# Moving a fused kernel's side work to other steps of its groups, and its agents' halves and key loads to other places

## The chip, the cores and the metric

One core of one Trainium2 chip runs the whole program. The metric is device time in microseconds (us) from the first to the last instruction of one execution, with what lies around them; the median of three runs is the figure for a kernel. TensorE is called PE here, VectorE DVE, ScalarE ACT, GpSimd POOL and SyncE, which issues the transfers, SP.

## What is computed

An attention over 49 agents (keys are folded into the agents, queries then read the agents), followed by a two-matrix layer with a leaky rectifier whose slope `alpha` differs by column. Two batches of 12480 tokens with 128 channels; the layer is 2048 wide.

```python
def attn(q, k, v, agents):                   # q, k, v: 2 x 12480 x 128; agents: 2 x 49 x 128
    a2k = softmax(scale * agents @ k.T)      # over all keys
    agent_v = a2k @ v                        # 49 x 128 per batch
    q2a = softmax(scale * q @ agents.T)      # over the 49 agents
    return q2a @ agent_v

def layer(x, w_in, w_out, alpha):            # w_in 128 x 2048, w_out 2048 x 128
    h = x @ w_in
    g = max(h, 0) + alpha * min(h, 0)
    return g @ w_out
```

## The kernel before

**Halves.** Most products run as sums of pairs of reduced-precision numbers: a value is split into a high part (written by ACT) and the rest (written by DVE as a difference). So `qh` and `ql` are a query group's halves, `ah` and `al` the agents', `rh` and `rl` those of the rectified layer input.

**Start (to about 105 us).** Keys of batch 0 come in 25 units `u` of 512 rows. Each unit is transposed on PE (`ktp`), copied by ACT (`kt`), multiplied with the agents (`kl`), and its scores copied out (`s`). Maxima, exponentials and the product with the values (`av`) follow in five spans of units. Between them DVE turns the weights, which arrive as 64-bit numbers, into 32-bit ones (`mag_win`, `wl` and their like). `prep_agents` (line 152) stands at the head of all this: for both batches it transposes the agents (`ag`) and makes `ah` with 8 copies on ACT and `al` with 4 differences and 4 copies on DVE.

**Loop.** Then 52 groups of 480 tokens follow, each in 8 steps (NM = 8); a step `s` handles 256 of the 2048 layer columns. In step `s` PE runs, in this order, `g1(s + 2)` (6 matmuls into `h`, from which ACT makes `rh` and DVE `rl`), then whatever the plan puts into the step, then `g2(s)` (12 matmuls that add `rh` and `rl` into `acc`). At a group's eighth step three more matmuls add the linear part (`zh`, `zl`), ACT copies one half of `acc` to `os` (line 829) and DVE adds the other (line 830). `h` has two buffers: `g1(s + 2)` overwrites what `rl` of step `s` has read, so it cannot start before that `rl` has ended. ACT, DVE, POOL and SP each run their instructions in the order in which the program states them.

**Shared banks.** Two PSUM bank pairs take turns as `acc`: a group uses one, and `pair_tile` (line 82) lends the other, which the group before has just left, to the work between: a query pair's logits (`lg`), its sums over the agents (`qsum`), the key products of batch 1 (`kl`, `av`), and the fold (`t1` to `ts`). Such a matmul must wait until DVE has added up `os` of the group before.

**The plan.** `at(s, f)` puts a function into step `s` after `g1`, `pre(s, f)` ahead of `g1`. Query groups are made in pairs, one for every 16 steps; `q_steps` (line 960) says at which step, counted from the pair's first, each link of the chain runs (transpose, halves, logits, copy, maximum on POOL, `q_sub` on DVE, two exponentials on ACT, the split, the sum, its way through memory as `qx`, the reciprocal). `hold` (line 981) finds two free steps for a use of the shared bank. Batch 1's keys (`kb`, four transfers a unit, three buffers) and values are spread over the first 26 groups, its fold over the groups after them. In `fold_tasks`, `rest` is the linear part: `tt` (16 matmuls), four `tm`, `tz` (16 matmuls) and `ts`, which makes `zh` and `zl`.

Below, "step 0 to 15" of a pair means its place in the 16 steps: a group ends with step 7, the next begins with step 8.

Of the kernel before, what the change touches and what calls it, by code (L numbers as in the profile page):

```python
# [10 lines left out]
F32R = mybir.dt.float32r  # L11
# [20 lines left out]
def kernel(  # L32
# [11 lines left out]
    nc = tc.nc  # L44
# [18 lines left out]
    NM = NF // 2  # L63
# [14 lines left out]
    TILES = ((0, HALF), (HALF, P))  # L78
# [73 lines left out]
    def prep_agents(b):  # L152
        t = ps_l.tile([P, 512], F32, tag="lg", name=f"agt_ps{b}")
        nc.tensor.transpose(t[:, 0:NA], agm[:, b, :], ident[0:NA, 0:NA])
        ag = per_b.tile([P, HALF], F32, tag="ag", name=f"ag{b}")
        nc.vector.tensor_copy(ag[:, 0:NA], t[:, 0:NA])
        nc.vector.tensor_copy(ag[:, NA:HALF], t[:, 0 : HALF - NA])

        ah, al = (
            per_b.tile([P, 2, 2, HALF], F32R, tag=n, name=f"{n}{b}") for n in ("ah", "al")  # L160
        )
        for h, (c0, c1) in enumerate(TILES):
            for r0, r1 in TILES:
                for d in range(2):
                    nc.scalar.copy(out=ah[r0:r1, h, d, :], in_=ag[c0:c1, :])
            for d in range(2):
                nc.vector.tensor_tensor(
                    out=al[c0:c1, h, d, :], in0=ag[c0:c1, :], in1=ah[c0:c1, h, d, :],
                    op=ALU.subtract,
                )  # L170
                r0, r1 = TILES[1 - h]
                nc.vector.tensor_copy(
                    al[r0:r1, h, d, :].bitcast(F32R), al[c0:c1, h, d, :]
                )
        st[b].update(ag=ag, ah=ah, al=al)

    raw = {}

# [681 lines left out]
    with tc.manual_schedule():  # L860
# [9 lines left out]
        for b in range(B):  # L870
# [3 lines left out]
            out=oma, in0=alp, scalar1=-1.0, scalar2=1.0, op0=ALU.mult, op1=ALU.add  # L874
# [7 lines left out]
        def at(s, f, *a):  # L882
            plan.setdefault(s, []).append((f, a))
# [7 lines left out]
        s = 0  # L891
# [17 lines left out]

        q0 = s - (NU - CUTS[-1])  # L910
        loads += [(q0 - 14, q_load, 0), (q0 - 4, q_load, 1)]
        for j, f in zip((-6, -5, -4, -2, -1, 0, 3, 3, 4, 4), q_chain[:10]):
            at(q0 + j, f, 0)
        for n in range(8):
# [42 lines left out]
        for f, i in zip(rest, (0, 0, 1, 1, 2, 3, 4)):  # L957
            at(i, f)

        q_steps = (-21, -20, -19, -15, -14, -14, -12, -11, -11, -9, -7, -6, -4)  # L960
        load = {}

        first = {}
# [1 line left out]
        def pre(s, f, *a):  # L965
            first.setdefault(s, []).append((f, a))
# [13 lines left out]

        def hold(s):

            while s in busy or s + 1 in busy or s % NM in (0, NM - 1):
                s += 1
            busy.update((s, s + 1))
            return s

        for i2 in range(NGT // 2):
            s0 = 2 * NM * i2
            if i2 == 0:  # L990
                at(9, q_sum, 0)
                pre(10, q_spread, 0)
                at(12, q_rec, 0)
                busy.update((0, 1, 2, 3, 4, 9, 10))
                continue
            steps = q_steps
            if i2 == 1:
                steps = (-14, -14, -13, -11, -10, -10, -8, -7, -7, -6, -5, -4, -3)
            else:
                at(max(0, s0 - 30), q_load, i2)  # L1000
            for i in (3, 10):
                busy.update((s0 + steps[i], s0 + steps[i] + 1))
            for f, i in zip(q_chain, steps):
                (pre if f in (q_take, q_spread) else at)(s0 + i, f, i2)
        for g in range(NGT):
            s0 = g * NM
            for i in range(NM):
                use(s0 + i, "dve", 0.57)
            for i in (7, 7, 0, 1):
                use(s0 + i, "act", 0.5)  # L1010
            at((g + 1) * NM + 3, o_take, g)
            at((g + 1) * NM + 6, o_scale, g)
            at((g + 1) * NM + 7, o_store, g)

        for b in range(1, B):
            base = (b - 1) * NG * NM
            parts = [(u, u + 2) for u in range(0, NU - 3, 2)] + [(NU - 3, NU)]
            assert NU % 2
            at(base + 8, k_begin, b, [(0, NU)], parts)
            s = base + 9  # L1020
            done = {}
            for c, (lo, hi) in enumerate([*parts[:-1], (NU - 3, NU - 1), (NU - 1, NU)]):
                us = tuple(range(lo, hi))
                for u in us:
                    s = fit(max(s, done.get(u - 3, 0) + 1), dve=0.57)
                    at(max(base, s - 9), load_kb, b, u)
                    at(s, k_transpose_dve, b, u)
                    s += 1
                t_log = hold(max(s + 1, done.get(lo - 1, 0) + 2))
                done.update((u, t_log) for u in us)  # L1030
                at(t_log, k_logits, b, us)
                pre(t_log + 1, k_take, b, us)
                use(t_log + 1, "dve", 0.4)
                if hi in (NU, *(p[1] for p in parts)):
                    t_max = fit(t_log + 2, dve=0.4)
                    at(t_max, k_max_keys, b, min(c, len(parts) - 1))
            s = t_max + 1
            at(s, k_max, b)
            s += 3
            done = {}  # L1040
            for lo, hi in parts:
                us = list(range(lo, hi))
                t_av = s
                for u in us:
                    s = fit(s, dve=0.3)
                    at(s, k_exp_a, b, u)
                    t_v = fit(max(s, done.get(u - 4, 0) + 1), act=0.5, dve=0.57)
                    at(max(base, t_v - 8), load_v1, b, u)
                    at(t_v, v_split, b, u)
                    t_e = fit(max(s + 1, done.get(u - 4, 0) + 1), act=0.5)  # L1050
                    at(t_e, k_exp_b, b, u)
                    t_c = fit(t_e + 1, dve=0.3)
                    at(t_c, k_exp_c, b, u)
                    t_av = max(t_av, t_c + 2, t_v + 2)
                t_av = hold(t_av)
                at(t_av, k_av2, b, us)
                pre(t_av + 1, k_add, b, us)
                use(t_av + 1, "dve", 0.5)
                for u in us:
                    done[u] = t_av  # L1060
            s = t_av + 2
            at(s, k_sum, b)
            lead, rest = fold_tasks(b)
            s += 2
            for f in lead:
                s = hold(s)
                at(s, f)
                s += 2
            while s % NM != 3 or any(s + i in busy for i in range(5)):
                s += 1  # L1070
            for f, i in zip(rest, (0, 1, 1, 2, 2, 3, 4)):
                at(s + i, f)
            busy.update(range(s, s + 5))
            s += 4
            assert s < base + (NG + 1) * NM - 1, (t_max, t_av, s, base + NG * NM)

        for s in range(NS):
# [41 lines left out]
```

## Time and profile before

| | us |
|---|---|
| median of three runs (lowest, highest) | 1112.08 (1108.16, 1114.1) |
| the profiled execution | 1114.53 |
| its span, first to last instruction | 1112.7 |
| PE busy in the span | 1059.0 |
| DVE busy | 820.3 |
| ACT busy | 634.1 |

PE is busy for 95% of the span, so the time is PE's own work and the places where it stands still. Matmuls overlap: the two row halves of one product run at once, and a step of 18 matmuls in loop takes about 2 us from one `h` to the next. A row that says `[0.39 <-DVE os L830]` means that the engine sat idle 0.39 us before this instruction and that DVE's line 830 ended the wait. The distance from one step's first `h` to the next shows a loss better than the idle time does, because the matmul pipeline has to fill again.

### The profile page before, as it was taken

To read this page: it belongs to the slowest core of one execution; us is meant where nothing else is said; L and a number is where in the kernel's file an instruction comes from. 1 tells how busy PE (TensorE), PEld (TensorE's weight loads), DVE (VectorE), ACT (ScalarE), POOL (GpSimd) and SP (SyncE) were. 2 spreads that over 40 slices of the span, in tenths; PEclk is the share of its full clock that TensorE was granted. 3 is DMA by queue.
4 is the path that set the end of the run, shared out by engine and by line. 5 is a ranking of instruction groups with operands and counts; after the bars stand their busy time and mean duration, and the time that the engine had idled before them with its cause. 6 is when DMAs were issued, how large, how long until landed. Compare 5 with 4: busy or idle time off the path is not lost.

```text
span 1112.7 us, 22465 instructions
## 1 busy us (share of the span) xinstructions
PE 1059.0 (95%) x9328; PEld 939.9 (84%) x9328; DVE 820.3 (74%) x1068; ACT 634.1 (57%) x807; POOL 109.9 (10%) x130
## 2 busy tenths in 40 slices
PE   7998969999999999999999899999999999999997
PEld 7985858877878878888878789899998899899997
DVE  5696557787786799899877577767777777777775
ACT  3354445555555567767656456666566665666653
POOL 1341101101101100110110110011101111011100
PEclk9989989999999999999999999999999999999999
DMA  9881013313323223233211111021211212112011
GB/s 264 221 185 28 1 31 64 57 30 65 57 39 50 47 57 76 60 73 70 37 28 23 24 29 33 15 37 30 35 29 19 37 28 38 21 27 37 10 20 28
DMA packets 305767, 57.25 MB, mean 51 GB/s; under 512 B 265567, under 2 KB 305153, under 8 KB 305665
## 3 DMA queue, kind: packets, MB, share of 16 engines
q1 hardware_dynamic: 304673, 55.69, 25.7%
q8 instruction: 73, 1.20, 0.4%
q14 instruction: 29, 0.24, 0.1%
q10 hardware_dynamic: 992, 0.12, 0.1%
HBM read 42.59 MB, written 12.78 MB: 50 GB/s over the span
## 4 chain that ended last, share of the span: by engine, by line
PE 62%; DVE 21%; ACT 10%; issue 4%; SPq 1%; DMA 1%; DVEq 0%; ACTq 0%; POOL 0%
PE acc L816 31%; PE h L794 16%; DVE rl L801 7%; ACT rh L800 5%; PE kl L372 4%; PE lg L713 3%; DVE qs L731 2%; ACT qmh L735 2%; ACT qs L740 2%; DVE qml L744 2%; PE av L527 2%; DVE ot L840 2%; DVE os L830 1%; PE qsum L755 1%; PE ktp L340 1%
## 5 line engine op out<-in xcount | busy, mean ns | idle before, releaser
L801 DVE SCALAR_TENSOR_TENSOR rl<-h,rh 128x960 fp32r<-128x960 f32 x416 | 476.5, 1150 | 236.4 <-ACT rh L800 235.7
L800 ACT ACTIVATE rh<-h 128x960 fp32r<-128x960 f32 x416 | 402.1, 971 | 322.6 <-PE h L794 314.2
L794 PE MATMUL h<-qmh,sab 64*128 64x480 f32 x1664 | 363.9, 384 | 5.9 <-DVE rl L801 4.9
L816 PE MATMUL acc<-rh,wl 64*128 64x480 f32 x1664 | 361.3, 382 | 1.5 <-DVE zl L663 1.2
L816 PE MATMUL acc<-rh,wh 64*128 64x480 f32 x1664 | 358.8, 378 | 0.0
L816 PE MATMUL acc<-rl,wh 64*128 64x480 f32 x1664 | 283.0, 379 | 0.0
L794 PEld LDWEIGHTS h<-qmh,sab 64*128 64x128 f32 x1664 | 207.0, 185 | 37.9 <-DVE rl L801 19.6
L816 PEld LDWEIGHTS acc<-rh,wl 64*128 64x128 f32 x1664 | 205.7, 185 | 20.2 <-issue 3.4
L816 PEld LDWEIGHTS acc<-rh,wh 64*128 64x128 f32 x1664 | 206.2, 185 | 14.2
L816 PEld LDWEIGHTS acc<-rl,wh 64*128 64x128 f32 x1664 | 189.0, 185 | 14.2
L794 PE MATMUL h<-qml,sab 64*128 64x480 f32 x832 | 190.6, 379 | 0.0
L726 POOL PARTITION_ALL_REDUCE qm<-qs x26 | 80.2, 3085 | 770.9 <-ACT qs L721 655.6
L794 PEld LDWEIGHTS h<-qml,sab 64*128 64x128 f32 x832 | 104.6, 186 | 6.0
L372 PEld LDWEIGHTS kl<-ag,kt 64*128 64x128 f32 (+2 forms) x588 | 58.8, 214 | 8.2 <-issue 3.8
L372 PE MATMUL kl<-ag,kt 64*128 64x49 f32 (+2 forms) x588 | 59.3, 293 | 5.3 <-ACT kt L344 2.9
L829 ACT COPY os<-acc 128x480 f32<-128x480 f32 x52 | 29.2, 561 | 32.4 <-PE acc L824 32.2
L762 ACT COPY qsum<-qsum 128x960 f32<-128x960 f32 x26 | 25.0, 961 | 19.2 <-DMA qx<-qsum 10.0
L830 DVE TENSOR_TENSOR os<-acc,os 128x480 f32<-128x480 f32 x52 | 33.5, 644 | 3.1 <-ACT os L829 3.0
L735 ACT ACTIVATE qmh<-qs,padb 128x960 fp32r<-128x960 f32 x26 | 28.6, 1099 | 11.0 <-DVE qs L731 10.7
L835 DVE STREAM_TRANSPOSE ot<-os 128x480 f32<-128x480 f32 x52 | 34.0, 653 | 0.0
L721 ACT COPY qs<-lg 128x960 f32<-128x960 f32 x26 | 25.0, 962 | 15.4 <-PE lg L713 14.1
L840 DVE TENSOR_TENSOR ot<-ot,qr 128x480 f32<-128x480 f32 x52 | 33.7, 648 | 0.0
(139 smaller groups left out, 892.9 us busy)
## 6 DMA issues: line engine op xcount, KB each, us to landing
qin<-in_q_dram SPq DMA_DIRECT2D x208, 60.0 KB, 2.1
out_dram<-ot SPq DMA_DIRECT2D x206, 60.0 KB, 1.9
v<-in_v_dram SPq DMA_DIRECT2D x12, 512.0 KB, 6.3
kb<-in_k_dram SPq DMA_DIRECT2D x96, 64.0 KB, 2.2
v<-in_v_dram SPq DMA_DIRECT2D x24, 256.0 KB, 2.8
k<-in_k_dram SPq DMA_DIRECT2D x11, 512.0 KB, 6.6
win<-in_moe_w_in_dram SPq DMA_DIRECT2D x4, 512.0 KB, 7.6
wo<-in_moe_w_out_dram SPq DMA_DIRECT2D x4, 512.0 KB, 6.8
```

What stands on the lines that cost most here:

```text
L372: nc.tensor.matmul(d[0:rows, c : c + NA], lhsT=kt[r0:r1, n * rows : (n + 1) * rows], rhs=st[b]["ag"][r0:r1, 0:NA], start=True, stop=True,)
L713: nc.tensor.matmul(t[:, i, 0:GT], lhsT=a[r0:r1, h].rearrange("p d a -> p (d a)"), rhs=x[r0:r1, h, :], start=n == 0, stop=n == len(jobs) - 1,)
L726: nc.gpsimd.partition_all_reduce(flat(t), flat(gq["s", k]), P, ReduceOp.max)
L735: nc.scalar.activation(out=m, in_=gq["s", k], func=AF.Exp, bias=padb, scale=SCALE)
L794: nc.tensor.matmul(h[:, u, 0:GT], lhsT=w[a][r0:r1, f0 : f0 + P], rhs=x[r0:r1, :], start=n == 0, stop=n == 2,)
L800: nc.scalar.activation(out=rh, in_=h[:, :, 0:GT], func=AF.Relu)
L801: nc.vector.scalar_tensor_tensor(out=rl, in0=h[:, :, 0:GT], scalar=0.0, in1=rh, op0=ALU.max, op1=ALU.subtract)
L816: nc.tensor.matmul(acc[:, i, 0:GT], lhsT=a[r0:r1, 2 * m + u, :], rhs=x[r0:r1, u, :], start=m == 0 and n == 0, stop=False,)
L829: nc.scalar.copy(out=t, in_=acc[:, 0, 0:GT])
L830: nc.vector.tensor_tensor(out=t, in0=acc[:, 1, 0:GT], in1=t, op=ALU.add)
L835: nc.vector.transpose(out=t.rearrange("p t i -> p (t i)"), in_=oo.pop(g))
L840: nc.vector.tensor_tensor(out=t, in0=t, in1=gq.pop(("r", g)).to_broadcast([P, TB, 32]), op=ALU.mult)
```

## The change

The query chain's numbers in `q_steps` move: logits from step 1 of a pair's place to step 2, the exponentials from step 5 to step 7, the split from step 7 to step 8, and sum, spread and reciprocal from before the pair begins to its own steps 10, 11 and 13. `hold` no longer gives out a group's second step. `o_scale` and `o_store` run one step later. `load_kb` and `load_v1` of a unit are stated only after the step in which the buffer's last unit was used. The agents' halves leave `prep_agents` for `prep_queries`, which is stated late in the start; its four copies across partitions run on POOL. Batch 1's linear part is cut in two: `tz` and `ts` get a hold of their own.

```diff
+    def prep_queries(b):
+        ag = st[b]["ag"]
...
         for h, (c0, c1) in enumerate(TILES):
-            for r0, r1 in TILES:
-                for d in range(2):
-                    nc.scalar.copy(out=ah[r0:r1, h, d, :], in_=ag[c0:c1, :])
+            r0, r1 = TILES[1 - h]
             for d in range(2):
+                nc.scalar.copy(out=ah[c0:c1, h, d, :], in_=ag[c0:c1, :])
+                nc.scalar.copy(out=ah[r0:r1, h, d, :], in_=ag[c0:c1, :])
                 nc.vector.tensor_tensor(
                     out=al[c0:c1, h, d, :], in0=ag[c0:c1, :], in1=ah[c0:c1, h, d, :],
                     op=ALU.subtract,
                 )
-                r0, r1 = TILES[1 - h]
-                nc.vector.tensor_copy(
-                    al[r0:r1, h, d, :].bitcast(F32R), al[c0:c1, h, d, :]
-                )
+                nc.gpsimd.tensor_copy(al[r0:r1, h, d, :], al[c0:c1, h, d, :])
...
+        at(q0 - 8, prep_queries, 0)
+        at(q0 + 1, prep_queries, 1)
...
-        q_steps = (-21, -20, -19, -15, -14, -14, -12, -11, -11, -9, -7, -6, -4)
+        q_steps = (-21, -20, -19, -14, -13, -13, -10, -9, -9, -8, 10, 11, 13)
...
-            while s in busy or s + 1 in busy or s % NM in (0, NM - 1):
+            while s in busy or s + 1 in busy or s % NM in (0, 1, NM - 1):
...
-                at(9, q_sum, 0)
-                pre(10, q_spread, 0)
-                at(12, q_rec, 0)
+                at(10, q_sum, 0)
+                pre(11, q_spread, 0)
+                at(13, q_rec, 0)
...
-                steps = (-14, -14, -13, -11, -10, -10, -8, -7, -7, -6, -5, -4, -3)
+                steps = (-16, -15, -14, -11, -10, -10, -8, -7, -7, -5, 10, 11, 13)
...
-            at((g + 1) * NM + 6, o_scale, g)
-            at((g + 1) * NM + 7, o_store, g)
+            at((g + 1) * NM + 7, o_scale, g)
+            at((g + 1) * NM + 8, o_store, g)
...
-                    at(max(base, s - 9), load_kb, b, u)
+                    at(max(base, s - 9, used.get(("k", u - 3), 0) + 1), load_kb, b, u)
+                    used["k", u] = s
...
-                    at(max(base, t_v - 8), load_v1, b, u)
+                    at(max(base, t_v - 8, used.get(("v", u - 3), 0) + 1), load_v1, b, u)
+                    used["v", u] = t_v
...
-            for f, i in zip(rest, (0, 1, 1, 2, 2, 3, 4)):
+            for f, i in zip(rest, (0, 1, 1, 2, 2)):
                 at(s + i, f)
-            busy.update(range(s, s + 5))
-            s += 4
+            busy.update(range(s, s + 4))
+            s = hold(s + 4)
+            at(s, rest[5])
+            at(s + 1, rest[6])
```

Three places show what stands where in the built program.

SP's queue in the first two groups, before (`kb1_1536` is batch 1's fourth key unit, `qx0` and `qx1` the first two pairs' sums on their way through memory):

```order
L332 DMA kb1_1024_1173<-in_k_dram 32x16x32 x4
L332 DMA kb1_1536_1334<-in_k_dram 32x16x32 x4
L332 DMA kb1_2048_1373<-in_k_dram 32x16x32 x4
L767 DMA qx0_1426<-qsum0_1424 30x1x32 x4
L767 DMA qx1_1495<-qsum1_1493 30x1x32 x4
L332 DMA kb1_2560_1566<-in_k_dram 32x16x32 x4
```

and now:

```order
L333 DMA kb1_1024_1175<-in_k_dram 32x16x32 x4
L333 DMA kb1_1536_1427<-in_k_dram 32x16x32 x4
L768 DMA qx0_1446<-qsum0_1444 30x1x32 x4
L333 DMA kb1_2048_1471<-in_k_dram 32x16x32 x4
L333 DMA kb1_2560_1574<-in_k_dram 32x16x32 x4
L851 DMA out_0_dram<-ot0_1467 32x15x32 x4
```

The fifth key unit's load now stands behind `qx0`, and `qx1` is gone from here: it follows 16 steps later.

ACT's queue around the end of group 34 (steps 7 and 8 of a pair; `rh282` belongs to step 10 of the pair), before:

```order
L800 ACTIVATE rh279_9967<-h279_9960 128x960
L735 ACTIVATE qmh18_9971<-qs18_9875,padb_85 128x960
L740 ACTIVATE qs18_9875<-qs18_9875,padb_85 128x960
L800 ACTIVATE rh280_9993<-h280_9986 128x960
L800 ACTIVATE rh281_10017<-h281_10010 128x960
L829 COPY os34_10042<-acc34_9826 128x480
L800 ACTIVATE rh282_10052<-h282_10045 128x960
```

and now:

```order
L801 ACTIVATE rh280_9971<-h280_9964 128x960
L801 ACTIVATE rh281_9995<-h281_9988 128x960
L736 ACTIVATE qmh18_9999<-qs18_9889,padb_85 128x960
L741 ACTIVATE qs18_9889<-qs18_9889,padb_85 128x960
L830 COPY os34_10018<-acc34_9808 128x480
L801 ACTIVATE rh282_10028<-h282_10021 128x960
```

The two exponentials now stand right ahead of the group's `os` copy and of `rh282`; before, two `rh` lay between.

DVE's queue around the end of group 8, while batch 1's keys are worked in, before:

```order
L801 SCALAR_TENSOR_TENSOR rl73_3447<-h73_3439,rh73_3446 128x960
L744 TENSOR_TENSOR qml5_3450<-qs5_3272,qmh5_3387 128x960
L354 STREAM_TRANSPOSE kt1_18_3456<-kb1_9216_3160 128x512
L830 TENSOR_TENSOR os8_3473<-acc8_3223,os8_3473 128x480
L801 SCALAR_TENSOR_TENSOR rl74_3484<-h74_3476,rh74_3483 128x960
```

and now:

```order
L802 SCALAR_TENSOR_TENSOR rl73_3418<-h73_3410,rh73_3417 128x960
L841 TENSOR_TENSOR ot7_3301<-ot7_3301,qr3_3105 128x480
L355 STREAM_TRANSPOSE kt1_17_3425<-kb1_8704_3134 128x512
L831 TENSOR_TENSOR os8_3442<-acc8_3205,os8_3442 128x480
L802 SCALAR_TENSOR_TENSOR rl74_3453<-h74_3445,rh74_3452 128x960
L745 TENSOR_TENSOR qml5_3456<-qs5_3286,qmh5_3421 128x960
L355 STREAM_TRANSPOSE kt1_18_3462<-kb1_9216_3200 128x512
```

The split (`qml5`) and a key transpose moved from ahead of the `os` sum to behind `rl74`, and the scale (`ot7`) and the key transpose `kt1_17` came from ahead of `rl73` to behind it.

## Rows read from the trace of the kernel before

**Rows 1.** The page: busy time by engine, and TensorE's granted clock in 40 slices.

```profile
PE 1059.0 (95%) x9328; PEld 939.9 (84%) x9328; DVE 820.3 (74%) x1068; ACT 634.1 (57%) x807; POOL 109.9 (10%) x130
...
PEclk9989989999999999999999999999999999999999
```

**Rows 2.** PE's longest wait: waiting line, releaser, us in total, times, longest.

```profile
PE qsum L755 <- DVE os L830: 16.3, 21, 1.5
```

**Rows 3.** PE and ACT in time, the start: start, length, line, operation, idle before.

```profile
7.75 1.97 PE L340 MATMUL ktp<-ident,k 128*128 128x128 f32 x8
12.61 0.67 PE L372 MATMUL kl<-ag,kt 128*128 128x49 f32 x2 [2.89 <-ACT kt L344]
...
10.35 1.60 ACT L165 CAST ah<-ag 64x64 fp32r<-64x64 f32 x8 [1.29 <-DVE ag L157]
```

**Rows 4.** DVE and POOL in time while weights are narrowed.

```profile
13.33 0.43 DVE L217 TENSOR_SCALAR mag_win<-mag_win 128x512 f32<-128x512 f32 x1
16.12 1.38 DVE L217 TENSOR_SCALAR mag_win<-mag_win 128x512 f32<-128x512 f32 x1
...
15.83 1.39 POOL L243 TENSOR_TENSOR win<-mag_win,win 128x512 f32<-128x512 f32 x1 [4.84 <-DVE win L236]
```

**Rows 5.** Steps 9 to 18 of the loop in time: PE, SP, ACT, PE.

```profile
136.66 0.58 PE L794 MATMUL h<-qmh,sab 64*128 64x480 f32 x2
174.15 0.38 PE L794 MATMUL h<-qmh,sab 64*128 64x480 f32 x2
...
140.69 8.49 SPq L332 DMA_DIRECT2D kb<-in_k_dram  x8
...
153.92 0.96 ACT L762 COPY qsum<-qsum 128x960 f32<-128x960 f32 x1 [10.04 <-DMA qx<-qsum]
...
155.03 1.99 PE L372 MATMUL kl<-ag,kt 64*128 64x49 f32 x32 [2.43 <-ACT qsum L762]
```

**Rows 6.** PE in time at a pair's step 9 while batch 1's keys are worked in.

```profile
352.08 0.48 PE L794 MATMUL h<-qmh,sab 64*128 64x480 f32 x2
...
354.31 0.48 PE L755 MATMUL qsum<-qml,ones 64*128 64x480 f32 x2 [1.31 <-DVE os L830]
```

**Rows 7.** PE, ACT and DVE in time, steps 5 to 9 of a later pair.

```profile
700.04 0.54 PE L794 MATMUL h<-qmh,sab 64*128 64x480 f32 x2
...
704.00 0.54 PE L794 MATMUL h<-qmh,sab 64*128 64x480 f32 x2
...
706.74 0.48 PE L794 MATMUL h<-qmh,sab 64*128 64x480 f32 x2
...
708.80 0.38 PE L794 MATMUL h<-qmh,sab 64*128 64x480 f32 x2
...
710.00 0.48 PE L755 MATMUL qsum<-qml,ones 64*128 64x480 f32 x2 [0.39 <-DVE os L830]
...
701.06 0.97 ACT L800 ACTIVATE rh<-h 128x960 fp32r<-128x960 f32 x1 [1.01 <-PE h L794]
702.35 1.10 ACT L735 ACTIVATE qmh<-qs,padb 128x960 fp32r<-128x960 f32 x1 [0.31 <-DVE qs L731]
703.54 1.10 ACT L740 ACTIVATE qs<-qs,padb 128x960 f32<-128x960 f32 x1
704.54 1.81 ACT L800 ACTIVATE rh<-h 128x960 fp32r<-128x960 f32 x2
706.77 0.56 ACT L829 COPY os<-acc 128x480 f32<-128x480 f32 x1 [0.41 <-PE acc L824]
...
701.16 1.15 DVE L731 TENSOR_TENSOR qs<-qs,qm 128x960 f32<-128x960 f32 x1
...
705.53 1.16 DVE L801 SCALAR_TENSOR_TENSOR rl<-h,rh 128x960 fp32r<-128x960 f32 x1 [2.15 <-ACT rh L800]
```

**Rows 8.** PE in time while batch 1's linear part is made.

```profile
628.37 3.71 PE L652 MATMUL z_ps<-wo,at 128*64 128x128 f32 x32 [1.78 <-DVE at L642]
...
637.89 0.49 PE L816 MATMUL acc<-rh,wl 64*128 64x480 f32 x2 [1.24 <-DVE zl L663]
```

More of the change, by code (lines that the diff above doesn't have):

```diff
@@ L157, in prep_agents @@
         nc.vector.tensor_copy(ag[:, NA:HALF], t[:, 0 : HALF - NA])
+        st[b].update(ag=ag)
+    def prep_queries(b):
+        ag = st[b]["ag"]
         ah, al = (
@@ L170, in prep_agents @@
                 )
-                r0, r1 = TILES[1 - h]
-                nc.vector.tensor_copy(
-                    al[r0:r1, h, d, :].bitcast(F32R), al[c0:c1, h, d, :]
-                )
-        st[b].update(ag=ag, ah=ah, al=al)
+                nc.gpsimd.tensor_copy(al[r0:r1, h, d, :], al[c0:c1, h, d, :])
+        st[b].update(ah=ah, al=al)
     raw = {}
@@ L990 @@
             if i2 == 0:
-                at(9, q_sum, 0)
-                pre(10, q_spread, 0)
-                at(12, q_rec, 0)
-                busy.update((0, 1, 2, 3, 4, 9, 10))
+                at(10, q_sum, 0)
+                pre(11, q_spread, 0)
+                at(13, q_rec, 0)
+                busy.update((0, 1, 2, 3, 4, 10, 11))
                 continue
@@ L1020 @@
             s = base + 9
-            done = {}
+            done, used = {}, {}
             for c, (lo, hi) in enumerate([*parts[:-1], (NU - 3, NU - 1), (NU - 1, NU)]):
@@ L1068 @@
                 s += 2
-            while s % NM != 3 or any(s + i in busy for i in range(5)):
+            while s % NM != 4 or any(s + i in busy for i in range(4)):
                 s += 1
-            for f, i in zip(rest, (0, 1, 1, 2, 2, 3, 4)):
+            for f, i in zip(rest, (0, 1, 1, 2, 2)):
                 at(s + i, f)
-            busy.update(range(s, s + 5))
-            s += 4
+            busy.update(range(s, s + 4))
+            s = hold(s + 4)
+            at(s, rest[5])
+            at(s + 1, rest[6])
+            s += 2
             assert s < base + (NG + 1) * NM - 1, (t_max, t_av, s, base + NG * NM)
```

## The prediction, made before the changed kernel ran

> **What bounds the kernel.** I read the page's busy times first: PE works 1059.0 us of the 1112.7 us span [rows 1], so about 54 us are its standing still, and an edit can only give back some of that. The list of PE's waits comes next: the one large item is the sum over the agents, which stands 21 times behind DVE's addition of the group before, 16.3 us in all [rows 2]. Then PE's stream in time, step by step, because a stall costs more than its idle time. The reader should see three kinds of loss: 2.89 us at the start [rows 3], one bad stretch in the loop's first groups [rows 5], and a loss that every pair of groups repeats [rows 6, 7]. A plain step is 1.98 us (700.04 to 704.00 is two of them).
>
> **1. The agents' halves.** The first key product waits 2.89 us for its `kt` copy, which stands on ACT behind 8 casts of 1.60 us that end at 11.95, and behind 8 more before those [rows 3]. The casts leave. The first transposes start at 7.75; their four are done about a microsecond later, half of the row of eight, and a copy of about 0.66 (11.95 to 12.61) lets the product start near 9.6: 3.0 us earlier. PE is then busy without a break for tens of microseconds and DVE's weight work follows PE's, so the shift travels. What comes back: 4 differences on DVE for batch 0 wait for 8 casts on ACT (1.60 us) at a place where DVE is packed; I charge 0.5, between 0 (hidden behind PE's products) and 1.6 (all on the path). Batch 1's stand where ACT and DVE have a gap; 0. The POOL copies are off the path unless they hold DVE up (rival B). Sum: **-2.5**, from -3.0 to -1.4.
>
> **2. Steps 9 to 18.** From 136.66 to 174.15 PE spends 37.5 us on nine steps [rows 5]. Their own work, two matmuls of 480 columns that run together taking a ninth of a plain step, 0.22: nine plain steps 17.8, two sums of two such pairs 0.9, a group's linear matmuls 0.2, logits of six pairs 1.3, and a key product 1.8 (its row of 1.99 less the overlap with what follows): 22.0. So 15.5 is lost. SP shows why: eight key transfers occupy it from 140.69 for 8.49 us, because the fifth unit waits for a buffer that DVE frees late; `qx0` stands behind them. ACT's copy of the second sum waits 10.04 us for `qx0` to be read, all `rh` behind it wait too, and PE's key product waits 2.43 us for that copy in turn [rows 5]. Now only four key transfers stand ahead of `qx0`, at half of the 8.49 us at most, and there is no second sum here. By the same order `qx0` is back some 3 us before DVE asks for it at step 13. What is late next: at step 11 DVE has the split, a query transpose, a result transpose and a key transpose in a row ahead of a `rl`; counted in its order that costs 0.4, and the starts of steps 12, 16 and 18 another 0.4 to 0.7 each, about 1.8 together. The moved sum saves its 0.44 here and pays it later. 15.5 less 1.8 is 13.7; the clock, which the page shows reduced in the slice that holds this stretch [rows 1], comes back with the stalls and is within that number. **-13.7**, from -15 to -8.
>
> **3. Every pair, the sum's wait.** After the first `h` of step 9 a sum should start 0.66 later (a third of a step). It starts 2.23 later while keys are worked in [rows 6], a loss of 1.57, and 1.20 later afterwards [rows 7], a loss of 0.54, both with about 0.1 for refilling. At step 10 the sum uses a bank whose addition ended long before. All of it goes.
>
> **4. Every pair, the exponentials.** Before, they sit at step 5 and cost 0.6: step 7's `h` is at 704.00 and step 8's at 706.74, 2.74 instead of the 2.18 of a step with its linear matmuls, since `rl` came only at 705.53 to 706.69 [rows 7]. Now they sit ahead of the `os` copy. I walk the new order with the old lengths, step 5's start as zero. `rh` starts 1.02 after its step's start and `rl` 1.0 later [rows 7]. `rl` of step 6 runs from 4.0 to 5.15; `q_sub` follows to 6.2 (DVE overlaps 0.1); the exponentials start at 6.25 and 7.44, ACT is free at 8.44 (703.54 to 704.54), the `os` copy ends at 9.0, `rh` of step 8's `h` at 9.9 to 10.1, and its `rl`, after scale and addition that fit in between, at 11.1 to 11.2. `h` of step 10 needs that `rl`. Without a wait it would start at 10.1 (four plain steps and one of 2.18). So step 10 begins 1.1 late, with the refill **1.2 a pair**, in place of 0.6. Bounds: 0.6, the old cost, and 2.3, both exponentials in full; I take the walk, since the old order walked in the same way gives the measured 706.74.
>
> Net for a pair: with keys, 0.6 and 1.7 leave, 1.2 comes, and the key transpose and the split that now follow the addition make the next `rl` about 0.3 late: -0.8, for about 8 pairs **-6.5**. Afterwards 0.6 and 0.64 leave and 1.2 comes: **-0.5** for 13 pairs, which is nothing.
>
> **5. The linear part.** The 16 `z` matmuls wait 1.78 us and the next group's accumulation 1.24 [rows 8]; with 0.3 each for refilling 3.6. With a hold of its own, `tz` comes some six steps after the last `tm`, `ts` three before its result is read. The three pairs in this stretch lose about 0.5 each by part 4. **-2.1**.
>
> Scale and store one step later, and the logits at step 2, cost nothing: the result tiles have two buffers, the pair's reciprocal stands two steps ahead. The values' loads wait for the same buffers as before, only without blocking SP.
>
> Sum: 2.5 + 13.7 + 6.5 + 0.5 + 2.1 = 25.3. From the profiled execution's 1114.5 that is 1089.2; the median of three lies 2.4 below that execution, so **1087**.
>
> **Rivals.** A, the first groups stay bad: SP still meets a key load that waits, or step 11's burst on DVE grows; for it speaks that `qx0` and key loads still alternate on one queue, against it that the second sum is gone. Half of part 2 is lost: 1094.
>
> B, POOL holds DVE up. A weight step of 0.43 us took 1.38 while POOL joined another slab from 15.83 to 17.22 [rows 4]. Four POOL copies now fall where DVE is packed; if each costs DVE 0.95 like that, 3.8 comes back and the start gains nothing: 1091. Against it: the copies are a sixteenth of the join's data. The Trainium skill, "SBUF — State Buffer", section "Who interferes with whom", states such a rule: DVE instructions with two inputs in SBUF, and copies and tensor-scalar steps in their two-port modes, take a port that GpSimd also uses, and whoever comes second is blocked for the whole instruction. By that rule rival B holds whenever a copy on POOL meets a two-input step on DVE, and here they stand close; the rows agree in kind, for the join.
>
> C, part 4 is worse: scale, addition or, in the groups with values, splits and exponent differences push that `rl` further. 0.7 more for 22 pairs: 1102. For it speaks that the new order packs exponentials, copy and `rh` without a gap; against it that `rl` falls only just behind `rh`. Its mirror, `rl` arriving 0.5 earlier, gives 1076.
>
> D, slower: the stall of over a microsecond at step 10, once in each of some 25 pairs, takes TensorE's clock from 2.4 to 1.2 GHz again and again. A step at the lower clock takes twice its 1.98 us, so 13 such steps eat the whole gain and from 16 on the kernel is over 0.5% slower; one for each pair gives 1087 + 25 x 2 = 1137. Against it: the wait of 1.31 us [rows 6] came back pair after pair and the page shows no clock loss in those slices [rows 1].
>
> **How the numbers follow.** Forecast 0.64, with its own range 1079 to 1096; A 0.12, B 0.09, C 0.12 with its mirror, D 0.03. The range 1076 to 1100 takes in A, B, the mirror and half of C. 0.5% is 5.6 us, about what a measurement of this kernel can tell from no change; faster by more means below 1106.5. Only D is above 1117.6, and a bad C with a bad start lies between: faster 0.94, same 0.03, slower 0.03.
>
> **What would show it.** The first key product near 9.6; steps 9 to 18 in about 24 us with no wait of ACT for `qx`; no wait of `qsum` for line 831; instead waits of `h` for `rl` of about a microsecond once in each pair, at step 10; no `z` wait. If PE waits for nothing at step 10, part 4 is wrong and the kernel faster than forecast; if SP's key loads still stand ahead of `qx` for 8 us, part 2 is.

## The result, and the profile after

The changed kernel takes **1083.31 us** (median of three, 1079.04 to 1084.57) against 1112.08; the ratio is 0.974, with a 95% interval from 0.968 to 0.980. The forecast was 1087, faster, so the direction and the size held: 28.8 us gained where the sum said 25.3. The profiled execution is the fastest of the three, 1079.04, with a span of 1077.2 us, so the trace shows 35.5 us less than that of before, 10 more than the sum; half of that lies at the start, where traces of one kernel differ too. Several of the prediction's terms got there by another way than it said.

The page's rows for busy time, with the granted clock in 40 slices:

```profile
PE 1042.8 (97%) x9328; PEld 934.0 (87%) x9328; DVE 821.4 (76%) x1060; ACT 630.1 (58%) x807; POOL 111.4 (10%) x138
...
PEclk7789999999999999999999999999999999999999
```

PE is busy 16 us less than in [rows 1], with the same 9328 matmuls. It stands still 34 us where it stood 54. A busy time that falls for equal work points at PE's clock, that is, at more work done at the higher of its two levels (2.4 and 1.2 GHz). Of the 16 us, 6.7 lie before step 0, where the lengths of equal products show the level (below; the row `PEclk` itself does not, see the last section), and 6.6 in steps 9 to 18, where the mean granted clock was 0.82 of full speed and is 1.00 now.

PE's longest wait inside the loop, from the list of waits (waiting line, releaser, us in total, times, longest):

```profile
PE h L795 <- DVE rl L802: 12.1, 26, 0.8
```

The row of [rows 2] is gone: no `qsum` waits any more. In its place `h` waits for `rl` once in each pair of groups, as forecast for step 10.

PE in time at the start:

```profile
9.00 1.09 PE L373 MATMUL kl<-ag,kt 128*128 128x49 f32 x8 [0.24 <-ACT kt L345]
...
14.57 1.08 PE L341 MATMUL ktp<-ident,k 128*128 128x128 f32 x4 [1.91 <-DMA k<-in_k_dram]
15.45 1.78 PE L373 MATMUL kl<-ag,kt 128*128 128x49 f32 x8
...
44.58 0.99 PE L373 MATMUL kl<-ag,kt 128*128 128x49 f32 x8
...
99.54 0.48 PE L795 MATMUL h<-qmh,sab 64*128 64x480 f32 x2
```

The first key product starts at 9.00 instead of 12.61 [rows 3]. Then PE waits for a key transfer. Eight key products take 1.09 us at first, 1.78 from 15.45 on, and 0.99 later. The last row is the `h` that begins step 0 of the loop (in the trace of before it begins at 106.94).

Steps 9 to 18 in time, PE (first and last `h`), then SP, then ACT:

```profile
129.27 0.58 PE L795 MATMUL h<-qmh,sab 64*128 64x480 f32 x2
...
151.15 0.49 PE L795 MATMUL h<-qmh,sab 64*128 64x480 f32 x2 [0.35 <-DVE rl L802]
...
133.31 1.91 SPq L333 DMA_DIRECT2D kb<-in_k_dram  x4
135.68 3.40 SPq L768 DMA_DIRECT2D qx<-qsum  x4
139.19 4.21 SPq L333 DMA_DIRECT2D kb<-in_k_dram  x8
...
134.67 0.95 ACT L763 COPY qsum<-qsum 128x960 f32<-128x960 f32 x1
```

21.9 us instead of 37.5 [rows 5]: ACT copies one sum, waits for nothing before it, and SP sends `qx` right behind.

Steps 9 and 10 of a later pair in time, PE, ACT and DVE, in the place of [rows 7]:

```profile
743.59 0.37 PE L795 MATMUL h<-qmh,sab 64*128 64x480 f32 x1
...
746.53 0.49 PE L795 MATMUL h<-qmh,sab 64*128 64x480 f32 x2 [0.48 <-DVE rl L802]
...
747.28 0.39 PE L756 MATMUL qsum<-qml,ones 64*128 64x480 f32 x2
...
742.87 1.10 ACT L741 ACTIVATE qs<-qs,padb 128x960 f32<-128x960 f32 x1
743.87 0.54 ACT L830 COPY os<-acc 128x480 f32<-128x480 f32 x1
744.31 1.84 ACT L801 ACTIVATE rh<-h 128x960 fp32r<-128x960 f32 x2
...
745.32 1.16 DVE L802 SCALAR_TENSOR_TENSOR rl<-h,rh 128x960 fp32r<-128x960 f32 x1 [0.22 <-ACT rh L801]
```

The `rl` that step 10 needs ends at 746.48 (745.32 and 1.16) and its `h` begins at 746.53: exponential, `os` copy, `rh`, `rl`, as the prediction walked it. The `h` before it begins at 743.59, so step 9 takes 2.94 us, 0.97 more than a plain step; over the last ten pairs the mean is 1.05, and 0.9 in most pairs with keys.

Where the 35.5 us of the traces went, by the starts of `h`:

| stretch | before | after | difference | forecast |
|---|---|---|---|---|
| to step 0 | 106.9 | 99.5 | -7.4 | -2.5 |
| steps 0 to 9 | 29.7 | 29.7 | 0.0 | |
| steps 9 to 18 | 37.5 | 21.9 | -15.6 | -13.7 |
| 18 to 144, batch 1's keys and values | 316.7 | 308.5 | -8.2 | -6.5 |
| 144 to 192 | 117.7 | 117.0 | -0.7 | |
| 192 to 208, linear part | 45.2 | 42.9 | -2.3 | -2.1 |
| 208 to the end | 459.0 | 457.7 | -1.3 | -0.5 |

Steps 9 to 18 don't hold the same work before and after. The third pair's logits (12 matmuls `lg`) stood in step 17, ahead of the `h` at 174.15 that begins step 18 [rows 5], and now stand in step 18, behind the `h` at 151.15. PE in time, before and now:

```profile
171.51 0.40 PE L713 MATMUL lg<-ql,ah 64*128 64x480 f32 x2
...
151.91 0.38 PE L714 MATMUL lg<-ql,ah 64*128 64x480 f32 x2
```

The second pair's sum has left these steps too. At the prediction's own prices, 1.3 and 0.44, some 1.7 of the 15.6 us is work that is now done behind step 18.

### The profile page after: what moved, and what is told of

It reads as the page before. It is cut to its first block, busy times and chain, and to the rows that moved or that the text cites. A ratio compares the mean times of both kernels' runs of the same rounds, so it can differ in the third digit from the quotient of the medians.

```text
span 1077.2 us, 22517 instructions
## 1 busy us (share of the span) xinstructions
PE 1042.8 (97%) x9328; PEld 934.0 (87%) x9328; DVE 821.4 (76%) x1060; ACT 630.1 (58%) x807; POOL 111.4 (10%) x138
## 4 chain that ended last, share of the span: by engine, by line
PE 64%; DVE 16%; ACT 12%; issue 5%; DMA 1%; SPq 1%; POOL 0%; DVEq 0%; ACTq 0%; POOLq 0%
PE acc L817 32%; PE h L795 19%; DVE rl L802 7%; ACT rh L801 5%; PE kl L373 3%; PE lg L714 3%; ACT qs L741 3%; ACT qmh L736 3%; DVE qs L732 2%; PE av L528 2%; PE av L561 1%; PE ktp L341 1%; ACT os L830 1%; DVE qml L745 1%; DVE ql L704 1%
## 5 line engine op out<-in xcount | busy, mean ns | idle before, releaser
L795 PE MATMUL h<-qmh,sab 64*128 64x480 f32 x1664 | 374.8, 384 | 14.1 <-DVE rl L802 12.1
L817 PE MATMUL acc<-rh,wl 64*128 64x480 f32 x1664 | 372.0, 380 | 0.0
L817 PE MATMUL acc<-rh,wh 64*128 64x480 f32 x1664 | 369.2, 377 | 0.0
L817 PE MATMUL acc<-rl,wh 64*128 64x480 f32 x1664 | 291.7, 378 | 0.0
L795 PEld LDWEIGHTS h<-qmh,sab 64*128 64x128 f32 x1664 | 215.1, 184 | 50.1 <-DVE rl L802 33.1
L817 PEld LDWEIGHTS acc<-rh,wl 64*128 64x128 f32 x1664 | 216.0, 184 | 17.5 <-issue 3.4
L817 PEld LDWEIGHTS acc<-rh,wh 64*128 64x128 f32 x1664 | 216.5, 184 | 12.9
L817 PEld LDWEIGHTS acc<-rl,wh 64*128 64x128 f32 x1664 | 198.6, 184 | 14.6
L795 PE MATMUL h<-qml,sab 64*128 64x480 f32 x832 | 198.7, 377 | 0.0
L831 DVE TENSOR_TENSOR os<-acc,os 128x480 f32<-128x480 f32 x52 | 33.6, 646 | 19.5 <-ACT os L830 19.5
L699 ACT CAST qh<-qt 128x960 fp32r<-128x960 f32 x26 | 25.9, 998 | 13.2 <-DVE qt L692 13.2
L736 ACT ACTIVATE qmh<-qs,padb 128x960 fp32r<-128x960 f32 x26 | 28.6, 1099 | 7.7 <-DVE qs L732 7.7
L722 ACT COPY qs<-lg 128x960 f32<-128x960 f32 x26 | 25.0, 960 | 12.1 <-PE lg L714 10.9
```

Source lines behind the costliest of these rows:

```text
L736: nc.scalar.activation(out=m, in_=gq["s", k], func=AF.Exp, bias=padb, scale=SCALE)
L795: nc.tensor.matmul(h[:, u, 0:GT], lhsT=w[a][r0:r1, f0 : f0 + P], rhs=x[r0:r1, :], start=n == 0, stop=n == 2,)
L817: nc.tensor.matmul(acc[:, i, 0:GT], lhsT=a[r0:r1, 2 * m + u, :], rhs=x[r0:r1, u, :], start=m == 0 and n == 0, stop=False,)
L831: nc.vector.tensor_tensor(out=t, in0=acc[:, 1, 0:GT], in1=t, op=ALU.add)
```

## Experiments

All ratios and medians are of timed executions against the kernel before on the same chip (medians of before there: 1111.8 to 1112.9); stretches are from one trace each. In the trace of the halves alone (below), whose plan for steps 9 to 18 is that of before, the stretch takes 33.6 us instead of 37.5, so one trace's stretch can be off by 4 us.

### Steps 9 to 18: the queue or the second sum

**Loads alone** (before, with this edit):

```
-                    at(max(base, s - 9), load_kb, b, u)
+                    at(max(base, s - 9, used.get(("k", u - 3), 0) + 1), load_kb, b, u)
+                    used["k", u] = s
...
-                    at(max(base, t_v - 8), load_v1, b, u)
+                    at(max(base, t_v - 8, used.get(("v", u - 3), 0) + 1), load_v1, b, u)
+                    used["v", u] = t_v
```

> The kernel before with one edit: a key or value load of batch 1 isn't issued before its buffer is free. Theory (SP's queue): qx of the first pair no longer stands behind eight key transfers, ACT's wait of 10.0 us for it goes, and steps 9 to 18 (136.66 to 174.15, 37.5 us before) take 23 to 26; the kernel is at 1098 to 1100. Rival (the sum's bank): the stretch is long because the first pair's sum is at step 9 on a bank that is still being read, and a second sum follows; then steps 9 to 18 stay over 33 us and the kernel over 1108.

1106.55 us, ratio 0.994 (0.992 to 0.996). Steps 9 to 18 take 29.7 us: half of the loss is gone, neither theory's number. ACT and PE in time there:

```profile
146.58 0.96 ACT L762 COPY qsum<-qsum 128x960 f32<-128x960 f32 x1 [2.96 <-DMA qx<-qsum]
...
145.16 0.77 PE L755 MATMUL qsum<-qml,ones 64*128 64x480 f32 x2 [3.40 <-DVE qml L744]
```

`qx` now stands ahead of the key transfers, and still the copy of the second sum waits 2.96 us for it, behind a second sum that itself waits 3.40 for its split.

**The first sum a step later, alone:**

```
-                at(9, q_sum, 0)
-                pre(10, q_spread, 0)
-                at(12, q_rec, 0)
+                at(10, q_sum, 0)
+                pre(11, q_spread, 0)
+                at(13, q_rec, 0)
```

> The kernel before with one edit: the first pair's sum at step 10, its spread at 11, its reciprocal at 13; the loads as before. Theory (SP's queue): qx comes a step later still, the key transfers stand in front of it as before, and steps 9 to 18 take 35 to 39 us; the kernel within 3 us of 1112. Rival (the sum's bank): steps 9 to 18 take 22 to 26 us and the kernel is at 1098 to 1100.

1114.26 us, ratio 1.002 (0.999 to 1.004); the stretch takes 37.2. The bank of the first sum is not the cause.

**Loads, and the second pair's sum 16 steps later** (both edits, the rest as before):

```
-                steps = (-14, -14, -13, -11, -10, -10, -8, -7, -7, -6, -5, -4, -3)
+                steps = (-16, -15, -14, -11, -10, -10, -8, -7, -7, -5, 10, 11, 13)
```

> The kernel before with two edits: loads not before their buffer is free, as in e2, and the second pair's table alone, which puts its sum at step 10 of its own groups instead of step 11 of the loop. Theory (two causes, half each): e2 left 29.7 us for steps 9 to 18, of which ACT's wait of 3.0 for qx, PE's wait of 3.4 for qml ahead of the second sum and a clock at the lower level after it remained; without the second sum these go, and the stretch takes 21.9 to 23.5 us, the kernel about 1099. Rival (the place of the first sum is needed too): the stretch stays over 27 us and the kernel over 1104.

1106.33 us, ratio 0.995 (0.993 to 0.997). The stretch takes 24.6, 1.1 above the theory's bound and below the rival's; the time, which the theory put at 1099, is on the rival's side and no better than with the loads alone. The 12.9 us won here are partly lost at once: steps 18 to 32 take 38.9 instead of 34.4, as the second pair's sum now meets the third's, which still has the old table.

**The second pair's table alone** (the diff just shown, with the loads as before):

> The kernel before with one edit: the second pair's table, which puts its sum 16 steps later; loads as before. Theory (two causes that add: SP's queue and the second sum): steps 9 to 18, 37.5 before, 29.7 with the loads alone and 24.6 with both, take 31 to 33 here. Rival 1 (the key transfers ahead of qx cost something only because a second sum's copy waits for qx): 24 to 26. Rival 2 (the queue is the whole cause, the second sum costs once it is gone): over 35. As in e5, some 5 us are lost again between steps 18 and 48, where the second pair's sum now meets the third's: 1106 to 1112 in all.

1108.92 us, ratio 0.998 (0.996 to 1.000). PE (first and last `h` of the stretch) and SP in time:

```profile
142.24 0.58 PE L794 MATMUL h<-qmh,sab 64*128 64x480 f32 x2
...
167.87 0.38 PE L794 MATMUL h<-qmh,sab 64*128 64x480 f32 x2
...
146.27 6.07 SPq L332 DMA_DIRECT2D kb<-in_k_dram  x8
152.45 3.40 SPq L767 DMA_DIRECT2D qx<-qsum  x4
```

25.6 us, with `qx` behind eight key transfers as before; all that is left of that queue is one wait, DVE's for `qx` (waiting line, releaser, us, times, longest):

```profile
DVE qst L775 <- DMA qx<-qsum: 1.2, 1, 1.2
```

So rival 1 holds. The queue is long either way; it stops ACT, and all `rh` behind it, only where a second sum's copy needs the buffer that `qx` is read from. The whole timed gain of this edit is small (3.0 us, with an interval that reaches 1), and in the trace steps 18 to 48 lose 6.4 of it again (34.4 and 40.4 before, 38.7 and 42.5 here): the collision of two sums, one pair later, with ACT's copy waiting 2.8 us for `qx` there. In one row: 37.5 before, 29.7 with the loads, 25.6 with the second sum moved (0.4 of it the sum's own work), 24.6 with both, 21.9 with the whole change. Of the last 2.7 us about half is the logits, which in these runs only the changed kernel has behind the stretch. The whole change without the edit of the loads was not run.

### The start

**The agents' halves late, alone** (the first edit of the change on the kernel before):

```
+    def prep_queries(b):
...
+                nc.gpsimd.tensor_copy(al[r0:r1, h, d, :], al[c0:c1, h, d, :])
...
+        at(q0 - 8, prep_queries, 0)
+        at(q0 + 1, prep_queries, 1)
```

> The kernel before with one edit of the change: the agents' halves are made late, the second half of al copied on POOL. Theory (the 16 casts alone): the first key product starts near 9.0 to 9.6 us instead of 12.61, and the loop's step 0, whose h(2) starts at 106.94 before, starts about 3 earlier, near 104: 1109.5 against 1112. Rival 1 (TensorE's clock): the earlier products let PE leave the lower of its two levels earlier too, as in the trace of the changed kernel, where 8 key products take 1.09 at first and 1.78 between 14.57 and 38.2, against 1.78 to 1.95 from 12.61 to 52.2 before: then step 0 is near 99.5 and the kernel at 1105. Rival 2 (chance): that stretch at the lower level ends at another time in each execution, whatever the halves: then the profile's step 0 lies anywhere between 99 and 107 and the times scatter by some 5 us. Rival 3 (POOL holds DVE up): step 0 stays at 106 or later.

1108.60 us (median of 12), ratio 0.997 (0.995 to 0.998), 3.9 less. In its trace step 0 begins at 97.71 and step 9 at 130.56, against 106.94 and 136.66. The time lies near the 1109.5 of the 16 casts alone, the trace beyond the 99.5 of rival 1; rival 3 is refuted.

**The same edit undone in the changed kernel, and the changed kernel once more:**

> The changed kernel with its first edit undone: the agents' halves are made at the start again. Theory (PE's level): in the trace step 0 goes back from 99.5 to 106.5 or later, because PE then works at the lower level from its first key product to about 50 us; the time goes up by 4 to 8, to 1087 to 1091. Rival 1 (the 16 casts alone): up by 2.5 to 3. Rival 2 (what comes earlier at the start is lost again in the loop's first steps): step 0 goes back, the time does not move by more than 1.

> The changed kernel as it is, beside e6 and e8 on the same chip: 1083 within 3 us. If PE's stretch at the lower level in the start ends by chance, the trace's step 0 lies away from 99.5 by more than 1 us; if the kernel sets it, within 0.5.

1085.37 us (median of six) and 1082.87 (median of five): 2.5 apart, as rival 1 had it, though the runs of each scatter over 8 us, so this pair alone doesn't settle the size. The traces have step 0 at 104.27 and 98.28, step 9 at 134.01 and 131.18; the theory's 106.5 was not reached. Step 0 of one and the same kernel lies 1.26 us apart in its two traces, so by the bound set ahead chance has a part in it. Everything after step 9 is alike to 0.5 us. Two things are seen in these traces. First, the lower level. Eight key products take 1.78 to 1.95 us until 52 us in the trace of before, until 43 in that of the halves early in the changed kernel, and until 38 in that of the changed kernel. In that of the halves alone they take 0.99 up to 25 us, and 0.99 again after 38; between, PE in time:

```profile
27.34 1.78 PE L373 MATMUL kl<-ag,kt 128*128 128x49 f32 x8
```

Second, the loop's first steps can lose as much. In the second trace of the changed kernel these run at the lower level in part, and steps 0 to 9 take 32.9 us instead of 29.7. Its row for a stretch (from and to, length, busy time and instructions of PE, PEld, DVE, ACT and POOL, granted clock, DMA share, GB/s; 1.00 is 2.4 GHz) has 0.70:

```profile
98.00:107.00 9.00, 8.06 (x45) 7.08 (x46) 4.17 (x6) 1.87 (x3) 0.00 (x0) 0.70 0.01 2
```

Three other traces lose the same 3.1 us there: two with the halves late (the halves alone is one) and one with them early.

With the halves late, seven traces have step 9 between 129.3 and 131.3 us; with the halves early, seven traces have it between 134.0 and 142.2, five of these between 136.4 and 137.8. How much of that is the casts and how much the level can be read from three traces in which PE makes equally many of these rows of eight products at the lower level before 52 us, eleven: the halves early in the changed kernel, and two further runs below with the halves late (the query's steps moved, and the scale a step earlier). The last slow row and step 0, of the first and the second:

```profile
38.24 1.78 PE L372 MATMUL kl<-ag,kt 128*128 128x49 f32 x8
...
104.27 0.48 PE L794 MATMUL h<-qmh,sab 64*128 64x480 f32 x2
```

```profile
35.23 1.78 PE L373 MATMUL kl<-ag,kt 128*128 128x49 f32 x8
...
101.06 0.48 PE L795 MATMUL h<-qmh,sab 64*128 64x480 f32 x2
```

Step 0 is 3.2 us earlier there, and 2.7 in the third (101.62): about the 3.0 of the casts. The rest of what the traces show is the number of slow rows: twelve or thirteen in the other six traces with the halves early, two to eight in the other five with them late. The seven kernels with the halves late have the same program up to step 0, so from two to eleven is chance; that eleven to thirteen with the halves early lies higher speaks for a part of the halves' place, and doesn't show it. The timed executions, whose medians are 2.5 to 3.9 us apart, have no trace.

### The pair's exponentials

**The two exponentials apart** (the changed kernel with this edit):

```
-        q_steps = (-21, -20, -19, -14, -13, -13, -10, -9, -9, -8, 10, 11, 13)
+        q_steps = (-21, -20, -19, -14, -13, -13, -11, -10, -8, -8, 10, 11, 13)
```

> The changed kernel with the two exponentials of a pair taken apart: difference at step -11, first exponential at -10, second at -8 beside the split (they were -10, -9, -9, -8). Theory (part 4, ACT's row of two exponentials and the os copy makes the stall at step 10): between the h of step 9 and that of step 10 there is no stall; a pair of groups takes 33.9 instead of 34.93 us, for 25 pairs about 25 us: 1058. Rival 1 (DVE): the split, addition and rl of that place are what is late; the stall stays or moves by a step, and under 5 us are gained. Rival 2 (place): an exponential at step 6 costs what the pair of them cost at step 5 before, 0.6 a pair; then 1068 to 1073.

**1066.33 us** (median of four), ratio 0.958 (0.955 to 0.961): 17 us below the changed kernel. ACT in time, steps 6 to 8 of a later pair:

```profile
729.00 1.10 ACT L736 ACTIVATE qmh<-qs,padb 128x960 fp32r<-128x960 f32 x1 [0.31 <-DVE qs L732]
730.00 0.95 ACT L801 ACTIVATE rh<-h 128x960 fp32r<-128x960 f32 x1
731.43 0.56 ACT L830 COPY os<-acc 128x480 f32<-128x480 f32 x1 [0.48 <-PE acc L825]
732.15 0.97 ACT L801 ACTIVATE rh<-h 128x960 fp32r<-128x960 f32 x1 [0.15 <-PE h L795]
733.02 1.09 ACT L741 ACTIVATE qs<-qs,padb 128x960 f32<-128x960 f32 x1
734.06 0.98 ACT L801 ACTIVATE rh<-h 128x960 fp32r<-128x960 f32 x1
```

Each exponential now fits nearly into the microsecond that ACT had free between two `rh`: the `rh` behind it starts 0.2 to 0.3 us later after its `h` than the 1.0 us of a plain step. PE's wait for `rl`, from the list of waits, 12.1 us in the changed kernel:

```profile
PE h L795 <- DVE rl L802: 1.6, 6, 0.4
```

The stall at step 10 is gone, as the theory had it, but its 1058 was too low: a pair takes 34.15 us (136.60 for four) instead of 34.91, not 33.9. The missing 0.25 is lost at steps 13 and 14, where DVE has a query's transpose, a result's transpose, the reciprocal and the difference in a row.

**The query's transpose, cast and difference a step later as well:**

> e4 with the query's transpose, cast and difference a step later as well (-20, -19, -18 in place of -21, -20, -19), so that DVE has one extra operation in each of the steps 11, 12, 13 and 14. Theory (the 0.2 us that e4 loses at step 13 and 0.1 at step 14 of each pair are DVE's row of two transposes, reciprocal and difference): both go, a pair takes 33.8 instead of 34.15 us, about 20 pairs give 5 to 6 us: 1060 to 1061 against 1066.3. Rival (the row only moves on, to the difference beside scale and addition at step 15): within 2 us of e4.

1064.96 us, ratio 0.959 (0.956 to 0.961), the same as the former within 1.4. The loss at step 13 is gone, and as much comes back in parts of 0.1 at steps 0 to 2, 8 and 10, and 0.25 more a pair at step 1 while keys are worked in. The rival holds.

**The exponentials back at step 5, the sum left at its new place:**

```
-        q_steps = (-21, -20, -19, -14, -13, -13, -10, -9, -9, -8, 10, 11, 13)
+        q_steps = (-21, -20, -19, -15, -14, -14, -12, -11, -11, -9, 10, 11, 13)
```

> The changed kernel with the pair's chain up to the split where it was before (-21, -20, -19, -15, -14, -14, -12, -11, -11, -9), so that both exponentials are at step 5 again; the sum stays at step 10 of the pair's own groups. Theory (part 4: the exponentials ahead of the os copy cost 1.05 to 1.15 a pair at step 10, at step 5 they cost 0.6 at steps 7 and 8): the stall at step 10 goes, that of before at steps 7 and 8 comes back, a pair takes 34.4 instead of 34.93 us, about 25 pairs give 11 to 14: 1069 to 1072. Rival (the stall at step 10 comes from the sum's new place, not from the exponentials): it stays, beside the old one, and the kernel is at 1090 to 1097.

1089.97 us, ratio 0.979 (0.975 to 0.982), 7 slower than the changed kernel. The theory's number is refuted; the rival's comes near, but not by its reason, as the rows show. In the later pairs 0.3 us of the stall at step 10 is left, in a pair with keys 1.4. From PE's list of waits:

```profile
PE h L795 <- DVE rl L802: 15.6, 17, 1.3
```

DVE and PE in time at the end of a group with keys:

```profile
250.47 1.14 DVE L745 TENSOR_TENSOR qml<-qs,qmh 128x960 fp32r<-128x960 f32 x1
251.52 0.65 DVE L841 TENSOR_TENSOR ot<-ot,qr 128x480 f32<-128x480 f32 x1
252.09 0.70 DVE L355 STREAM_TRANSPOSE kt<-kb 128x512 f32<-128x512 f32 x1
252.72 0.62 DVE L831 TENSOR_TENSOR os<-acc,os 128x480 f32<-128x480 f32 x1
253.26 2.21 DVE L802 SCALAR_TENSOR_TENSOR rl<-h,rh 128x960 fp32r<-128x960 f32 x2
...
254.46 0.49 PE L795 MATMUL h<-qmh,sab 64*128 64x480 f32 x2 [1.31 <-DVE rl L802]
```

No sum waits for the addition, yet PE stands still as long, now for the `rl` behind that addition. A pair with keys takes 40.17 us, as before the change (40.37), against 39.13 in the changed kernel. The sum is no part of that chain. So with the exponentials at step 5 its wait for the `os` addition was how DVE's lateness showed, not a cost of its own: behind the exponentials the `rl` and the split come late, DVE works on without a gap (250.47 to 255.47), and whoever asks first pays. This kernel differs from that of before in the loads, `hold`, the scale, the halves and the linear part as well, and the edit the other way round, the sum alone put back in the changed kernel, was not run.

**The same with the scale a step earlier:**

```
-            at((g + 1) * NM + 7, o_scale, g)
-            at((g + 1) * NM + 8, o_store, g)
+            at((g + 1) * NM + 6, o_scale, g)
+            at((g + 1) * NM + 7, o_store, g)
```

> e9 with one more edit undone: the result's scale at step 6 and its store at 7 of the next group, as before the change. Theory (in e9 DVE's row of split, scale, addition and, while keys are worked in, a key transpose makes the rl late that step 10 needs: PE waits 1.31 us for it at 254.46): without the scale that stall shrinks by the scale's 0.65 us; a pair with keys takes 39.4 to 39.6 us instead of 40.17, a pair without 34.5 instead of 34.84; the whole about 6 us under e9's profile of 1090 if PE's level is alike, 1080 to 1085. Rival (the exponentials at step 5 are the whole of it): pairs stay at 40.1 and 34.8, and the kernel is within 2 of e9.

1089.97 us, ratio 0.980 (0.977 to 0.983); pairs take 40.17 and 34.87 us, to 0.03 those of the former. What steps 1 and 9 of a pair with keys win by it (0.3 and 0.1 us), steps 0 and 8 lose. The theory's single culprit is refuted. That the amount of queued work counts is what the rows suggest.

### The linear part alone

```
-            for f, i in zip(rest, (0, 1, 1, 2, 2, 3, 4)):
+            for f, i in zip(rest, (0, 1, 1, 2, 2)):
...
+            s = hold(s + 4)
+            at(s, rest[5])
+            at(s + 1, rest[6])
```

> The kernel before with one edit: the linear part of batch 1 in two holds. Theory (part 5): PE's waits of 1.78 us ahead of the z products and of 1.24 ahead of the next group's accumulation go, and the 16 steps around it (192 to 208, 45.2 us) take 42 to 43.7; the rest as before. Rival (at, z and the abs copies are late in any order): over 44.5.

One execution, 1112.92 us, within the scatter. In the trace steps 192 to 208 take 43.0 us instead of 45.2, and the products begin without a wait:

```profile
638.83 3.71 PE L652 MATMUL z_ps<-wo,at 128*64 128x128 f32 x32
```

The theory holds in that trace: -2.2.

## Why the prediction was right, and where not

**Part 1, the agents' halves: the mechanism right, the trace's size not.** The first key product was forecast near 9.6 and came at 9.00. The 2.5 us are near what the timed kernels show (2.5 and 3.9) and what traces with equally many slow rows show (2.7 and 3.2). The traces that differ by this edit alone show 4.7 to 9.2 at step 0, because PE also left the lower level earlier in those with the halves late, by chance in part. The price of "an earlier PE" was worked out at one speed, although the row of 1.97 us for eight transposes [rows 3] stood in a trace that makes four of them in 1.08 us until 49 us and in 0.62 later.

**Part 2, steps 9 to 18: the number right, the weights wrong.** -13.7 forecast, -15.6 measured, or -13.9 on equal work. That the stretch now takes 21.9 us, as the 22.0 of own work, is luck: the logits and the second sum have left it, so its own work is 20.3, and 1.6 are lost, near the 1.8 forecast for "what is late next" (0.4 in step 11, 0.4 in step 13, 0.6 in step 17). The prediction left the logits in, although the change names their new step. The failed step is "SP shows why". The eight key transfers were named the cause and the second sum came second. Alone, the second sum's new place takes 11.9 us off, the transfers' order 7.8, and both together 12.9: each breaks the same chain, the second sum breaks more of it.

**Part 3, the sum's wait: wrong as a cost of its own.** "All of it goes" is true of the row and not of the time. With the exponentials at their old place, the sum's move gave 0.2 us a pair with keys and 0.2 without, not 1.57 and 0.54, and the wait came back as 15.6 us of `h` waiting for `rl`. What the move is worth once the exponentials stand late was not measured.

**Part 4, the exponentials: right in itself, and part of part 3 seems to belong here.** The stall at step 10 was forecast at 1.2 a pair and measured at 1.05 (0.9 with keys), by the chain that was walked. But 0.6 as the old place's price was too low, most likely since DVE's lateness behind it had been booked to the sum: with the sum moved away, the old place costs 0.55 and 0.09 at steps 7 and 8, and 0.30 and 0.09 at steps 9 and 10, 1.0 in all in a later pair. As the two errors have opposite signs, the net held nearly, and partly by luck: -0.8 forecast and -1.2 measured in a pair with keys, -0.04 and -0.1 later.

**Part 5** was forecast at -2.1 and measured at -2.3, alone -2.2.

**The rivals.** A did not come. C's mirror came in part, for pairs with keys. D did not: the stall stands in each pair and the page shows no slice below 9 tenths after the third. B's mechanism is there, and no cost of it was seen. The Trainium skill, "SBUF — State Buffer", section "Who interferes with whom", says that the engine that comes second at the port shared by DVE and GpSimd is blocked for the whole instruction. The trace agrees, with POOL as the one that waits: of its eight copies (231 to 1380 ns, median 236) one, in the group of four from 85.86 on, took 1.38 us while DVE worked on the queries' difference, 1.14 us from 86.61, and it ended 0.1 behind that difference, at 87.85. The traces of the other kernels with the halves late have the same copy at 1.38. In the other direction one of DVE's eight differences took 1.02 us instead of 0.22 (83.57 to 84.59) while POOL ran an all-reduce, which the kernel before has too; by the profile that ran until 85.79, so the difference was not held for the whole of it. No instruction is listed as waiting for the copies, and step 0 came earlier than forecast.

## What to carry to other kernels

A wait shows who paid, not what was late: before a wait is booked as a gain, ask what the waiting engine would meet next without it, and whether the engine it waited for was behind its own work. Extra work on an engine that has a gap of a microsecond in each step was nearly free here in single pieces of that length, and cost about a microsecond as soon as two stood together; taken apart they gave 17 us, more than any single edit of the change that was timed alone. A stretch between two fixed steps is compared only after counting what work it holds on either side. Where two collisions sit in one chain, either edit alone can seem to be the cause, so undo both ways before sharing the gain out; here that was done for steps 9 to 18, and not for the sum and the exponentials.

## What the chip showed that was not expected

The granted clock can read full where PE is not. In the stretch from 14.5 to 38 us the changed kernel's row and that of before have the same 23.5 us of PE at the same length of products (1.78 us for eight), with 0.50, the lower of the two levels, in the first and 1.00 in the second (columns as above):

```profile
14.50:38.00 23.50, 23.43 (x111) 22.37 (x111) 14.14 (x25) 8.64 (x20) 6.19 (x8) 0.50 1.15 318
```

```profile
14.50:38.00 23.50, 23.50 (x115) 23.07 (x114) 14.92 (x25) 9.13 (x21) 6.46 (x8) 1.00 1.06 298
```

The start of the kernel with the loads alone is that of before, with the same lengths, and its row reads 0.50. So the length of a known product is the better clock there. And the same kernel takes its stretches at the lower level at different places: of two traces of the changed kernel one lost 3.2 us in steps 0 to 9, where its clock read 0.70, and the other none.
